# Two tile groups of the first layer norm turned by DMA, and a four-layer kernel's orders laid out anew

## The chip, the cores and the metric

The kernel runs on one core of a Trainium2 chip, in one launch. The metric is the device time of one execution in microseconds, and the figure for a kernel is the median of its timed runs. TensorE is called PE here, VectorE DVE, ScalarE ACT, GpSimd POOL, and SyncE, which issues the DMAs, SP.

## The reference

Two linear-attention layers and two feed-forward layers alternate on x (1 x 2048 x 512, bf16), each with a layer norm in front and a residual behind it.

```python
def _A_ref(x, wqkv, wo):                      # attention, 32 heads of 16
    q, k, v = ...                             # x @ wqkv
    phi = lambda t: jnp.where(t > 0, t + 1, jnp.exp(t)) + 1e-6
    pq, pk = phi(q), phi(k)
    kv = jnp.einsum("bhsd,bhse->bhde", pk, v)
    z = jnp.einsum("bhsd->bhd", pk)
    num = jnp.einsum("bhqd,bhde->bhqe", pq, kv)
    den = jnp.einsum("bhqd,bhd->bhq", pq, z)[..., None] + 1e-6
    ...                                       # (num / den) @ wo
def _B_ref(x, w1, w2):                        # relu(x @ w1) @ w2, inner width 1376
    ...
x = A_x
x = x + _A_ref(_layernorm(x, axis=-1), A_wqkv, A_wo)
x = x + _B_ref(_layernorm(x, axis=-1), B_w1, B_w2)
x = x + _A_ref(_layernorm(x, axis=-1), A_wqkv, A_wo)
x = x + _B_ref(_layernorm(x, axis=-1), B_w1, B_w2)
```

## The kernel before

The 2048 tokens are 16 tiles of 128, in four chunks of four tiles (chunk 0 is tiles 0 to 3, chunk 1 is 4 to 7). The layers are numbered 0 to 3, and an operation's name carries its layer (`0.kproj6`).

**Layer 0, a tile's way.** A chunk of x is loaded to `xin` (`ld_x`). DVE takes mean and variance (`bnst`, `bnag`, L476 and L477) and adds the epsilon (`veps`), POOL raises it to the power of -1/2 (`rstd`, L883 for a single tile of chunk 0, L491 for two tiles of chunk 1; ACT does it for chunks 2 and 3), and DVE scales (`norm`, L519) into `xn`. For matmuls the tile must be turned, 512 features by 128 tokens, into `Tb`. In `transpose_pe` PE does that with four matmuls of 128 x 128 against an identity (`trp`, L556), and ACT or DVE takes the result out of PSUM (`trev`, L560 and L561). In `transpose_chunk` a DMA does it (`tr`, L539, issued by SP). `FIRST_PE_CHUNKS = 2` sends chunks 0 and 1 to PE and chunks 2 and 3 to DMAs. Chunk 0 goes faster: its tiles are only centred (`cent`, L887) before they are turned, and the factor `rstd` enters when the products leave PSUM; the scaled copy in `xn` (L932) follows later.

From `Tb` come k (`kproj`, one group of four 512-column matmuls a tile, `a_k`) and q (`qtok` by tile in chunk 0, `qproj` by feature block in the others, `a_q`). `phi_evac` brings them through phi: ACT writes a linear part (`_lin`, L583) and an exponential (`_exp`, L585), DVE takes a minimum (`_em`, L587) and a maximum (`_phi`, L594). With a name in `STT`, DVE does the linear part within the maximum (L591).

**The product with pk.** The kernel does not compute v. `a_g` multiplies the transpose of `xn` with pk = phi(k) and adds over all 16 tiles in PSUM (`g<half>_<block>_<chunk>`, 256 columns, or 512 for block 3, which also gives the sums z through a column of ones that POOL writes into `xn`, `onec`). The result, `GT`, meets `wv` (`kv`, then `kvmask`) and `wo` (`m`), which gives `Mf`. The denominators (`den`, 32-column matmuls) go through Ln and Exp on ACT (`lnd`, `rdc`) and are spread over partitions by DMAs (`spread`); DVE multiplies them into pq (`pqs`), and pq times `Mf` gives the layer's output (`fin`), to which `resid` adds x. wv is changed before use by subtracting its last row (`wvless`), which waits for `ld_wv` and `ld_wvl`.

**What sets the order.** Every operation is put in a graph with what it reads and writes and an assumed duration, and `_list_schedule` lays out each engine's queue: among operations that could start at once, the smaller priority comes first. `HINTS` moves the priority of single operations, and `SEQS` fixes the order of some at the head. At run time each engine works its queue in order and waits on semaphores. All matmuls but the turning and warm ones are recorded at L601.

**The head.** Before data are there PE runs nine 512-column matmuls on a zeroed tile `wrm` (L451, `warm`) and one of 256 columns (L454, `warm2`), which DVE's memset (L444) releases. SP issues the loads in this order: tile 0 of x, tiles 1 to 3, two halves of wk, chunk 1, wq, chunks 2 and 3, wv (L432), the last row of wv (L433), wo (L434); then the transposes.

Of the kernel before, what the change touches and what calls it, by code (L numbers as in the profile page):

```python
# [9 lines left out]
BF16 = mybir.dt.bfloat16  # L10
# [5 lines left out]
C_MM512 = 216.0  # L16
C_MM256 = 109.0
C_MM128 = 57.0
C_MM96 = 42.5
C_MM_SWITCH = 95.0  # L20
C_MMTINY = 30.0
C_ACT_PSUM = 495.0
# [25 lines left out]

HINTS = {"2.zcol": 36, "2.norm0": -300, "2.norm1": -300, "2.norm2": -300, "2.norm3": -300, "0.bnag8": 9, "0.bnst11": -2, "0.bnst12": 58, "0.den1": 288, "0.fin11_0": 83, "0.fin8_0": 93, "0.g0_2_0": 180,
# [6 lines left out]

SEQS = {
    "dve": ["bnst0", "bnag0", "cent0", "bnst2", "bnst1", "bnag2", "cent3", "bnag1", "cent2", "trev0b"],
    "act": ["mean_3", "trev0a", "sq_3", "trev3", "trev2", "trev1"],
    "pool": ["veps_0", "rstd_0", "veps_2", "veps_1", "rstd_1", "var_3"],  # L60
    "pe": ["trp0a", "warm2"],
}

STT = {"0.k10", "0.k6", "0.k9", "0.q3_2", "0.q3_3"}


class _Op:
    __slots__ = ("eng", "emit", "reads", "writes", "dur", "lat", "sdeps", "odeps", "idx",
                 "seq", "dma", "name", "t_start", "t_done", "issued", "pos", "alts", "late", "prio", "key", "lock")

    def __init__(self, eng, emit, reads, writes, dur, lat, dma, name):
        self.eng = eng
        self.emit = emit
        self.reads = reads
        self.writes = writes
        self.dur = dur
        self.lat = lat
        self.dma = dma
        self.name = name
        self.sdeps = []  # L80
        self.odeps = []
        self.alts = None
        self.seq = None
        self.t_start = None
        self.t_done = None
        self.issued = False
        self.late = 0.0
        self.lock = eng == DVE and dur < 345.0 and (name.endswith(("_em", "_phi")) or name[:4] in ("cent", "norm", "wvle"))


class _Graph:

    def __init__(self):
        self.ops = []
        self.last_w = {}
        self.readers = {}
        self.tile_ops = {}
        self.ntiles = 0
        self.layer = 0

# [5 lines left out]
    def add(self, eng, emit, reads=(), writes=(), dur=100.0, lat=0.0, dma=False, name=""):  # L106
        op = _Op(eng, emit, tuple(reads), tuple(writes), dur, lat, dma, name)
        op.idx = len(self.ops)
        op.key = "%d.%s" % (self.layer, name)
        op.prio = op.idx + HINTS.get(op.key, 0)  # L110
        deps = {}
# [36 lines left out]
def _list_schedule(ops, tile_ops, vbank, nbanks=8):  # L148
# [44 lines left out]
    while remaining:  # L193
# [45 lines left out]
        o.issued = True  # L239
        o.t_start = st  # L240
        for v in alloc_of.get(o.idx, ()):
            bsel = None
# [49 lines left out]
def build_kernel(nc, A_x, A_wqkv, A_wo, B_w1, B_w2, out, n_layers_pairs=2, A_PE_CHUNKS=0, windows=None,  # L292
                 WARM=9, SPLIT0=True, TAIL_SPLIT=True, LAST_HALVES=True, FIRST_PE_CHUNKS=2,
                 flex_strict=True, flex_bias_dve=0.0):
# [18 lines left out]
    with es:  # L313
# [41 lines left out]
        nhalf = sb("nhalf", [128, 4], F32)  # L355
        wrm = sb("wrm", [128, 512], BF16)
        onesf = sb("onesf", [128, 128], F32)
# [65 lines left out]
        wq_v = A_wqkv.rearrange("(c p) n -> p c n", p=128)  # L423
        ld_x(0, 1, lat=1550.0)
        for k in range(2):
            dma(lambda e, k=k: e.dma_start(wqkv[:, 2 * k:2 * k + 2, D:2 * D], wq_v[:, 2 * k:2 * k + 2, D:2 * D]),
                [], [("wk", k)], 1050.0 + 150.0 * k, "ld_wk%d" % k)
        ld_x(1, lat=1450.0)
        dma(lambda e: e.dma_start(wqkv[:, :, 0:D], wq_v[:, :, 0:D]), [], [("wq",)], 1550.0, "ld_wq")
        for t in range(2, NCH):  # L430
            ld_x(t)
        dma(lambda e: e.dma_start(wqkv[:, :, 2 * D:3 * D], wq_v[:, :, 2 * D:3 * D]), [], [("wv0",)], 1500.0, "ld_wv")  # L432
        dma(lambda e: e.dma_start(wvl[:], A_wqkv[D - 1:D, 2 * D:3 * D].broadcast_to([128, D])), [], [("wvl",)], 1850.0, "ld_wvl")  # L433
        dma(lambda e: e.dma_start(wo[:], A_wo.rearrange("(c p) n -> p c n", p=128)), [], [("wo",)], 1650.0, "ld_wo")  # L434
        nfull = NFC - 1 if FLAST < 128 else NFC
# [8 lines left out]
        g.add(DVE, lambda e: e.memset(wrm[:], 0.0), [], [("wrm",)], 150, name="ms_wrm")  # L444
        if WARM > 0:
            wt = alloc_bank()

            def _warm(e):
                last = None
                for k in range(WARM):  # L450
                    last = e.matmul(psv[:, wt, :], wrm[:, 0:128], wrm[:, :], start=True, stop=True)  # L451
                return last
            g.add(PE, _warm, [("wrm",)], [("ps", wt)], WARM * 427.0, name="warm")
            g.add(PE, lambda e: e.matmul(psv[:, wt, 0:256], wrm[:, 0:128], wrm[:, 0:256], start=True, stop=True),  # L454
                  [("wrm",)], [("ps", wt)], 213.0, name="warm2")
        g.add(POOL, lambda e: e.memset(onesf[:], 1.0), [], [("onesf",)], 200, name="ms_ones")
# [87 lines left out]
        def transpose_pe(i):  # L544
            dst = Tb[:, i, :, :].rearrange("p c t -> p (c t)")

            def part(c0, n, key, tag):
# [5 lines left out]
                def _emit(e):  # L553
# [3 lines left out]
                    return last  # L557
                g.add(PE, _emit, [("xn", i), ("ident",)], [("ps", b)], n * (107.0 if i in (0, 3) else C_MM128), name="trp" + tag)
                d = dst[:, 128 * c0:128 * (c0 + n)]
                act = (ACT, lambda e: e.activation(d, psb()[:, :], ACTF.Identity), C_ACT_PSUM if n == 4 else 300.0)  # L560
                dve = (DVE, lambda e: e.tensor_copy(d, psb()[:, :]), 400.0 if n == 4 else 270.0)  # L561
                alts = [act, dve] if n == 4 else [act] if c0 == 0 else [dve]
                g.add_flex(alts, [("ps", b)], [key], name="trev" + tag)
# [57 lines left out]
        def a_k(i):  # L621
            b = alloc_bank()
            for c0, n, key, tag in ((0, 2, "T0a", "a"), (2, 2, "T", "b")) if i == 0 and g.layer == 0 else ((0, 4, "T", ""),):
                mm_group(lambda c0=c0, n=n: [(psv[:, b, :], Tb[:, i, c, :], wqkv[:, c, D:2 * D], c == 0, c == 3, False)
                                             for c in range(c0, c0 + n)],
                         [(key, i)] + [("wk", k) for k in range(c0 // 2, (c0 + n) // 2)], [("ps", b)], n * C_MM512, "kproj%d%s" % (i, tag))
            phi_evac(b, pk_tile(i), ("big", pk_unit(i)), "k%d" % i,
                     tok=i if g.layer == 0 and i < 4 else None)
# [18 lines left out]

        def a_g(m, i0, n, hf, GB, col, opens, width=256):
            def mk():
                mms = []  # L650
                for i in range(i0, i0 + n):
# [4 lines left out]
            mm_group(mk, [("xn", i) for i in range(i0, i0 + n)] + [("big", pk_unit(i)) for i in range(i0, i0 + n)],  # L656
                     [("ps", GB)], n * (C_MM256 if width == 256 else C_MM512), "g%d_%d_%d" % (hf, m, i0 // 4))

# [232 lines left out]
        def ln_first(t):  # L891
            if t == 0:
# [69 lines left out]
        def layer_steps(layer):  # L962
# [3 lines left out]
            if layer % 2 == 0:  # L966
# [237 lines left out]
```

## Time and profile before

| | before |
|---|---|
| timed runs, us | 280.75, 281.76, 282.42 |
| median, us | 281.76 |
| profiled execution, us | 280.62 |
| its span in the trace, us | 278.9 |
| PE busy, of the span | 98% |
| ACT, DVE, POOL busy | 61%, 52%, 17% |

The span runs from the first to the last instruction recorded; the rest of the profiled execution's time, 1.72 us, lies around it. In rows of the timeline the first number is the start and the second how long the row lasts, both in us; a row with xN is N instructions in one, and the bracket behind it is the engine's idle time before it and what ended that. Busy times of PE overlap from one matmul to the next, so the pace of matmuls is read from start to start.

### The profile page before, as it was taken

The numbers are of one execution on the slowest core, as the hardware profiler recorded it, in microseconds if no ns is written. First come the engines' busy times: TensorE is split into PE (matmuls) and PEld (weight loads), VectorE is DVE, ScalarE is ACT, GpSimd is POOL, SyncE is SP. The second block draws the span as 40 slices with busy tenths as digits, with TensorE's granted clock in tenths as the row PEclk, the third lists the DMA queues.
The fourth block names the chain that finished last, engine by engine and source line by source line (L and its number), as shares of the span: only waits on it lengthen the run. The fifth ranks groups of instructions, "written<-read, shape, count | busy, mean of one in ns | idle before, by whom it ended". The sixth has DMA issues, their size and how long they took to land.

```text
span 278.9 us, 4192 instructions
## 1 busy us (share of the span) xinstructions
PE 272.7 (98%) x1551; PEld 140.4 (50%) x1573; DVE 144.4 (52%) x385; ACT 169.5 (61%) x351; POOL 47.9 (17%) x131
## 2 busy tenths in 40 slices
PE   6999999999999999999999999999999999999996
PEld 2545656546544544544454455764654554454443
DVE  5999982899501362443363477379966300120222
ACT  4999787758773682678372799765683366226000
POOL 5500000044500160400040400005236100000000
PEclk9999999999999999999999999999999999999999
DMA  7922397655750043070006030084313641021012
GB/s 214 379 55 53 75 251 254 150 130 76 144 47 0 2 94 75 1 96 0 0 2 76 0 75 2 6 200 99 76 38 59 165 80 21 0 75 22 0 75 75
DMA packets 46356, 22.62 MB, mean 81 GB/s; under 512 B 36640, under 2 KB 44800, under 8 KB 46336
## 3 DMA queue, kind: packets, MB, share of 16 engines
q1 hardware_dynamic: 46336, 22.35, 35.3%
q8 instruction: 12, 0.20, 0.3%
q14 instruction: 8, 0.07, 0.1%
HBM read 7.14 MB, written 2.10 MB: 33 GB/s over the span
## 4 chain that ended last, share of the span: by engine, by line
PE 95%; DMA 1%; ACT 1%; issue 1%; DVE 1%; SPq 0%
PE ps L601 95%; DMA xin<-in_A_x_dram 1%; PE ps L556 1%; ACT big L583 1%; ACT escr L585 0%; DVE bst L476 0%; SPq L420 0%; DVE xn L932 0%; DVE xin L850 0%; DVE xn L887 0%; DVE mv L477 0%
## 5 line engine op out<-in xcount | busy, mean ns | idle before, releaser
L601 PE MATMUL ps<-w,big 128*128 128x512 bf16 (+4 forms) x355 | 76.2, 373 | 0.4
L601 PE MATMUL ps<-Tb,w 128*128 128x512 bf16 (+1 forms) x352 | 70.8, 360 | 0.0
L601 PEld LDWEIGHTS ps<-w,big 128*128 128x128 bf16 (+1 forms) x363 | 35.1, 98 | 41.1
L830 ACT ACTIVATE big<-ps 128x512 bf16<-128x512 f32 x67 | 40.0, 597 | 23.8 <-PE ps L601 23.5
L618 ACT ACTIVATE sqscr<-xres 128x512 bf16<-128x512 f32 x48 | 29.9, 623 | 36.5 <-DVE xres L612 36.2
L601 PEld LDWEIGHTS ps<-Tb,w 128*128 128x128 bf16 x352 | 33.9, 98 | 32.8
L612 DVE SCALAR_TENSOR_TENSOR xres<-ps,xres 128x512 f32<-128x512 f32 x32 | 21.2, 689 | 40.5 <-PE ps L601 40.5
L609 DVE TENSOR_TENSOR xin<-ps,xres 128x512 bf16<-128x512 f32 x15 | 10.4, 691 | 49.7 <-PE ps L601 49.7
L583 ACT ACTIVATE big<-ps 128x512 bf16<-128x512 f32 x51 | 32.0, 631 | 5.3 <-PE ps L601 5.3
L601 PE MATMUL ps<-wqkv,Tb 128*128 128x512 bf16 x138 | 32.6, 379 | 1.4 <-ACT Tb L560 1.0
L601 PE MATMUL ps<-big,xn 128*128 128x256 bf16 (+1 forms) x222 | 30.6, 287 | 0.1
L585 ACT ACTIVATE escr<-ps 128x512 bf16<-128x512 f32 x44 | 27.9, 636 | 1.0 <-PE ps L601 1.0
L601 PE MATMUL ps<-Tb,wqkv 128*128 128x512 bf16 x112 | 26.5, 379 | 0.1
L601 PEld LDWEIGHTS ps<-big,xn 128*128 128x128 bf16 x224 | 21.6, 98 | 8.8 <-issue 0.4
L601 PE MATMUL ps<-Mf,big 128*128 128x512 bf16 x109 | 24.8, 379 | 0.2
L587 DVE TENSOR_SCALAR escr<-escr 128x512 bf16<-128x512 bf16 x52 | 14.7, 290 | 17.8 <-ACT escr L585 17.8
L499 POOL TENSOR_SCALAR mean<-s 128x4 f32<-128x4 f32 (+1 forms) x13 | 3.1, 238 | 117.3 <-DVE xres L612 117.1
L601 PEld LDWEIGHTS ps<-wqkv,Tb 128*128 128x128 bf16 x144 | 13.8, 98 | 16.8 <-ACT Tb L560 1.2
L594 DVE TENSOR_TENSOR big<-big,escr 128x512 bf16<-128x512 bf16 x49 | 20.4, 421 | 1.1
L523 DVE TENSOR_SCALAR xn<-xres,mean,rstd 128x512 bf16<-128x512 f32 x24 | 16.1, 706 | 4.6 <-POOL nbias L513 4.3
L601 PEld LDWEIGHTS ps<-Mf,big 128*128 128x128 bf16 x112 | 10.7, 98 | 13.1 <-DVE big L755 0.4
L601 PEld LDWEIGHTS ps<-Tb,wqkv 128*128 128x128 bf16 x112 | 10.9, 98 | 11.6
(94 smaller groups left out, 227.8 us busy)
## 6 DMA issues: line engine op xcount, KB each, us to landing
big<-rdc SPq DMA_DIRECT2D x32, 128.0 KB, 2.7
xin<-in_A_x_dram SPq DMA_DIRECT2D x3, 512.0 KB, 7.4
w<-in_B_w_dram SPq DMA_DIRECT2D x1, 1376.0 KB, 7.9
w<-in_B_w_dram SPq DMA_DIRECT2D x1, 1280.0 KB, 10.7
wqkv<-in_A_wqkv_dram SPq DMA_DIRECT2D x2, 512.0 KB, 7.9
out_dram<-xin SPq DMA_DIRECT2D x2, 512.0 KB, 2.8
wqkv<-in_A_wqkv_dram SPq DMA_DIRECT2D x2, 256.0 KB, 4.1
wo<-in_A_wo_dram SPq DMA_DIRECT2D x1, 512.0 KB, 9.1
```

The source lines that it names most:

```text
L499: g.add(POOL, lambda e: e.tensor_scalar(mean[:, sl], s1[:, sl], -INV_D, None, ALU.mult), [("s1", i) for i in tl], [("mean", i) for i in tl ...
L523: ts = (POOL, lambda e: e.tensor_scalar(xn[:, i, :], src, mean[:, i:i + 1], rstd[:, i:i + 1], ALU.add, ALU.mult), C_POOL_NORM)
L556: last = e.transpose(psb()[:, 128 * c:128 * c + 128], xn[:, i, 128 * (c0 + c):128 * (c0 + c) + 128], ident[:])
L583: g.add(ACT, lambda e: e.activation(dst_ap, psv[:, b, :], ACTF.Identity, bias=1.0 + 1e-6, scale=sc), [("ps", b)] + rk, [dst_key], C_ACT_PS ...
L585: g.add(ACT, lambda e: e.activation(esc, psv[:, b, :], ACTF.Exp, scale=sc), [("ps", b)] + rk, [ekey], C_ACT_EXP + xd, name=name + "_exp")
L587: g.add(DVE, lambda e: e.tensor_scalar(esc, esc, 1.0, 1e-6, ALU.min, ALU.add), [ekey], [ekey], C_DVE_BF4X, name=name + "_em")
L594: g.add(DVE, lambda e: e.tensor_tensor(dst_ap, dst_ap, esc, ALU.max), [dst_key, ekey], [dst_key], 340.0, name=name + "_phi")
L601: last = e.matmul(o, l, r, start=st, stop=sp, skip_group_check=skip)
L609: g.add(DVE, lambda e: e.tensor_tensor(xin[:, i, :], psv[:, b, :], src, ALU.add), [("ps", b), skey], [("xin", i)], C_DVE_PSUM, name="resid ...
L612: g.add(DVE, lambda e: e.scalar_tensor_tensor(xres[:, i, :], psv[:, b, :], 0.0, src, ALU.add, ALU.add, accum_out=s1[:, i:i + 1]), [("ps", ...
L618: g.add(ACT, lambda e: e.activation(sqscr[:, q, :], xres[:, i, :], ACTF.Square, accum_out=s2[:, i:i + 1]), [("xres", i)], [("sqscr", q), ( ...
L830: g.add_flex([(ACT, lambda e, M=M, b=b, u=u: e.activation(unit_ap(u, M), psv[0:M, b, :], ACTF.Relu), C_ACT_PSUM), (DVE, lambda e, M=M, b=b ...
```

## The change

- `FIRST_PE_CHUNKS` is 1: chunk 1 is scaled and then turned by two DMAs of two tiles (`tr1_1` for tiles 6 and 7, `tr1_0` for 4 and 5, in that order on SP), and chunks 2 and 3 by two each. Sixteen turning matmuls and four evictions go. Chunk 1's statistics come in the order 6, 7, 4, 5.
- Chunk 0's part of the first product is cut in two pairs, tiles 0 and 2, then 3 and 1 (`g0_3_0p0` and so on). PE's queue: k of tiles 0, 3, 2, the turn of tile 1, q of 0 and 2, k of 1, q of 3 and 1, products of the first pair, k of 6, products of the second pair with others, k of 7, products, k of 4 and 5.
- wv, its last row and wo are issued behind chunk 1's transposes.
- The warm matmuls read a constant tile of ones that exists at the start, so nothing is waited for: eight of 512 columns, the turn of half of tile 0, five of 256 columns, the turn of the other half. Both evictions of tile 0 are on ACT, and the first k projection comes behind the turns of tiles 3 and 2.
- `HINTS`, `SEQS`, `STT` and some assumed durations are new, and with them all orders; of those far from the head, `den0`, `den1` and `den2` of layer 0 now stand together on PE, and in layer 2 the priorities of the first norms are gone.

```diff
-                 WARM=9, SPLIT0=True, TAIL_SPLIT=True, LAST_HALVES=True, FIRST_PE_CHUNKS=2,
+                 WARM=8, SPLIT0=True, TAIL_SPLIT=True, LAST_HALVES=True, FIRST_PE_CHUNKS=1,
...
-        dma(lambda e: e.dma_start(wqkv[:, :, 2 * D:3 * D], wq_v[:, :, 2 * D:3 * D]), [], [("wv0",)], 1500.0, "ld_wv")
...
-        g.add(DVE, lambda e: e.memset(wrm[:], 0.0), [], [("wrm",)], 150, name="ms_wrm")
...
+            one_w = nc.const_aps.tensor(1.0, [128, 128], BF16)
+            one_m = nc.const_aps.tensor(1.0, [128, 512], BF16)
...
+            warm([512] * WARM, "warm")
+            warm([256], "warm2")
+            for k in (3, 4, 5, 6):
+                warm([256], "warm%d" % k)
...
-            step = 2 if t < FIRST_PE_CHUNKS else 4
+            step = 2 if t < 2 else 4
...
-                tr_dma(t, 2 if t == 2 else 1)
+                tr_dma(t, 2)
+                if t == 1:
+                    load_out_weights(g.ops[-2:])
...
-        FIRST_ORDER = (0, 3, 1, 2)
+        FIRST_ORDER = (0, 2, 3, 1)
+        G_PAIRS = (FIRST_ORDER[:2], FIRST_ORDER[2:])
...
+                def g_pair(k):
+                    a_g(3, k, 2, 0, GR, 0, True, 512)
+                    for m in range(3):
+                        a_g(m, k, 2, 0, GA[m // 2], 256 * (m % 2), m % 2 == 0)
...
-                    if t >= 1:
+                    if t == 1 and first_layer:
+                        for k in range(len(G_PAIRS)):
+                            g_pair(k)
+                    elif t >= 1:
                         g_r(t - 1)
                         g_a(t - 1)
```

More of the change, by code (lines that the diff above doesn't have):

```diff
@@ L20 @@
 C_MM_SWITCH = 95.0
+C_DEN = 218.0
+T_CLK = 5600.0
 C_MMTINY = 30.0
@@ L98, in __init__ @@
         self.ntiles = 0
+        self.keys = set()
         self.layer = 0
@@ L240, in _list_schedule @@
         o.t_start = st
+        if e == PE:
+            if o.key.startswith("0.den"):
+                o.dur = C_DEN if order[PE][-1].name.startswith("den") else C_DEN + 2 * C_MM_SWITCH
+            o.wdur = o.dur
+            if st < T_CLK and o.key[:5] in ("0.trp", "0.kpr"):
+                o.dur *= 2.0
         for v in alloc_of.get(o.idx, ()):
@@ L443, in _table, with warm, _warm @@
             return e.activation(lnw[:], nhalf[:, 0:2], ACTF.Square)
-        g.add(DVE, lambda e: e.memset(wrm[:], 0.0), [], [("wrm",)], 150, name="ms_wrm")
         if WARM > 0:
             wt = alloc_bank()
[L448 to L455, printed above, removed]
+            one_w = nc.const_aps.tensor(1.0, [128, 128], BF16)
+            one_m = nc.const_aps.tensor(1.0, [128, 512], BF16)
+            def warm(cols, name):
+                def _warm(e):
+                    last = None
+                    for n in cols:
+                        last = e.matmul(psv[:, wt, 0:n], one_w, one_m[:, 0:n], start=True, stop=True)
+                    return last
+                g.add(PE, _warm, [], [("ps", wt), ("wrm",)], sum(cols) / 1.2, name=name)
+            warm([512] * WARM, "warm")
+            warm([256], "warm2")
+            for k in (3, 4, 5, 6):
+                warm([256], "warm%d" % k)
         g.add(POOL, lambda e: e.memset(onesf[:], 1.0), [], [("onesf",)], 200, name="ms_ones")
@@ L622, in a_k @@
             b = alloc_bank()
[L623 removed]
+            for c0, n, key, tag in ((0, 2, "T0a" if i == 0 else "T", "a"), (2, 2, "T", "b")) if i in FIRST_ORDER[:2] and g.layer == 0 else ((0, 4, "T", ""),):
                 mm_group(lambda c0=c0, n=n: [(psv[:, b, :], Tb[:, i, c, :], wqkv[:, c, D:2 * D], c == 0, c == 3, False)
                                              for c in range(c0, c0 + n)],
[L626 removed]
+                         [(key, i)] + [("wk", k) for k in range(c0 // 2, (c0 + n) // 2)] + ([("wrm",)] if g.layer == 0 else []), [("ps", b)], n * C_MM512, "kproj%d%s" % (i, tag))
             phi_evac(b, pk_tile(i), ("big", pk_unit(i)), "k%d" % i,
@@ L648, in a_g @@
         def a_g(m, i0, n, hf, GB, col, opens, width=256):
+            tl = range(i0, i0 + n) if n == 4 else G_PAIRS[i0]
             def mk():
                 mms = []
-                for i in range(i0, i0 + n):
+                for i in tl:
                     u = pk_unit(i)
@@ L655, in mk @@
                 return mms
-            mm_group(mk, [("xn", i) for i in range(i0, i0 + n)] + [("big", pk_unit(i)) for i in range(i0, i0 + n)],
-                     [("ps", GB)], n * (C_MM256 if width == 256 else C_MM512), "g%d_%d_%d" % (hf, m, i0 // 4))
+            mm_group(mk, [("xn", i) for i in tl] + [("big", pk_unit(i)) for i in tl],
+                     [("ps", GB)], n * (C_MM256 if width == 256 else C_MM512), "g%d_%d_%d" % (hf, m, i0 // 4) + ("" if n == 4 else "p%d" % i0))
         def a_g_evac_row(GR):
@@ L917, in ln_first, with load_out_weights @@
             if t >= FIRST_PE_CHUNKS:
-                tr_dma(t, 2 if t == 2 else 1)
+                tr_dma(t, 2)
+                if t == 1:
+                    load_out_weights(g.ops[-2:])
             ones_col(t)
-        FIRST_ORDER = (0, 3, 1, 2)
+        def load_out_weights(after):
+            n = len(g.ops)
+            dma(lambda e: e.dma_start(wqkv[:, :, 2 * D:3 * D], wq_v[:, :, 2 * D:3 * D]), [], [("wv0",)], 1500.0, "ld_wv")
+            dma(lambda e: e.dma_start(wvl[:], A_wqkv[D - 1:D, 2 * D:3 * D].broadcast_to([128, D])), [], [("wvl",)], 1850.0, "ld_wvl")
+            dma(lambda e: e.dma_start(wo[:], A_wo.rearrange("(c p) n -> p c n", p=128)), [], [("wo",)], 1650.0, "ld_wo")
+            for o in g.ops[n:]:
+                o.odeps.extend(after)
+        FIRST_ORDER = (0, 2, 3, 1)
+        G_PAIRS = (FIRST_ORDER[:2], FIRST_ORDER[2:])
         tr_state = {"first": True}
```

33 lines of the change are left out of this document (17 added, 16 removed), and 16 rows, old and new, of the table HINTS.

## The prediction

> **What bounds the kernel now.** I read the busy table first, then the chain that ended last, then the waits of TensorE (PE), and last the timeline of the first 20 us.
>
> ```profile
> PE 272.7 (98%) x1551; PEld 140.4 (50%) x1573; DVE 144.4 (52%) x385; ACT 169.5 (61%) x351; POOL 47.9 (17%) x131
> PE 95%; DMA 1%; ACT 1%; issue 1%; DVE 1%; SPq 0%
> PE ps L451 <- DVE wrm L444: 1.2, 1, 1.2
> PE ps L601 <- ACT Tb L560: 1.0, 1, 1.0
> PE ps L556 <- DVE xn L887: 0.3, 1, 0.3
> ```
>
> PE is busy for 98% and carries 95% of the chain. The three waits are all it has, and all lie ahead of 7 us. So from there on the kernel is one unbroken row of matmuls: a change can win what it removes from PE's work or from the head, and loses every wait that it brings in. Other engines matter only where they make PE wait.
>
> ```profile
> 1.24 3.40 PE L451 MATMUL ps<-wrm 128*128 128x512 bf16 x9 [1.24 <-DVE wrm L444]
> 2.92 0.15 PEld L451 LDWEIGHTS ps<-wrm 128*128 128x128 bf16 x1 [0.28 <-issue]
> 3.35 0.15 PEld L451 LDWEIGHTS ps<-wrm 128*128 128x128 bf16 x1 [0.28 <-issue]
> 4.97 0.63 ACT L897 ACTIVATE sqscr<-xin 128x512 bf16<-128x512 bf16 x1 [2.42 <-DMA xin<-in_A_x_dram]
> 4.97 1.29 DVE L476 BATCH_NORM_STATS2 bst<-xin 128x6 f32<-128x512 bf16 x2 [0.78 <-DMA xin<-in_A_x_dram]
> 5.60 0.36 ACT L560 ACTIVATE Tb<-ps 128x256 bf16<-128x256 bf16 x1
> 6.02 0.60 PE L601 MATMUL ps<-wqkv,Tb 128*128 128x512 bf16 x2 [1.05 <-ACT Tb L560]
> 6.17 0.40 DVE L932 TENSOR_SCALAR xn<-xin,mv,rstd 128x512 bf16<-128x512 bf16 x1
> 6.49 0.17 DVE L477 BATCH_NORM_AGGREGATE mv<-bst 128x2 f32<-128x6 f32 x1
> 6.58 0.32 DVE L887 TENSOR_SCALAR xn<-xin,mean 128x512 bf16<-128x512 bf16 x1
> 6.91 0.32 DVE L887 TENSOR_SCALAR xn<-xin,mv 128x512 bf16<-128x512 bf16 x1
> 6.96 0.72 PE L556 MATMUL ps<-ident,xn 128*128 128x128 bf16 x8 [0.34 <-DVE xn L887]
> 7.52 0.59 PE L601 MATMUL ps<-wqkv,Tb 128*128 128x512 bf16 x2
> 8.17 5.34 PE L601 MATMUL ps<-wqkv,Tb 128*128 128x512 bf16 x23
> ```
>
> The head is set by data: tiles 1 to 3 of x land, DVE takes their statistics from 4.97, centres tile 3 at 6.58 and tile 2 at 6.91, and PE turns them at 6.96. At 8.17 PE has turned four tiles and done one k projection; after that it never stops.
>
> **The change, part by part.** Prices of steady PE work, and of the handed-over steps:
>
> ```profile
> 15.53 0.61 PE L556 MATMUL ps<-ident,xn 128*128 128x128 bf16 x8
> 15.97 2.75 PE L601 MATMUL ps<-wqkv,Tb 128*128 128x512 bf16 x12
> 29.80 1.03 PE L601 MATMUL ps<-Tb,wqkv 128*128 128x512 bf16 x4
> 30.67 1.04 PE L601 MATMUL ps<-big,xn 128*128 128x256 bf16 x8
> 31.54 1.03 PE L601 MATMUL ps<-Tb,wqkv 128*128 128x512 bf16 x4
> 8.40 1.29 DVE L476 BATCH_NORM_STATS2 bst<-xin 128x6 f32<-128x512 bf16 x2 [0.19 <-DMA xin<-in_A_x_dram]
> 11.11 0.16 DVE L483 TENSOR_SCALAR veps<-mv 128x2 f32<-128x2 f32 x1
> 11.35 1.66 POOL L491 TENSOR_TENSOR rstd<-veps,nhalf 128x2 f32<-128x2 f32 x2 [1.61 <-DVE mv L477]
> 12.57 0.72 DVE L519 TENSOR_SCALAR xn<-xin,mv,rstd 128x512 bf16<-128x512 bf16 x2
> 19.37 0.75 DVE L594 TENSOR_TENSOR big<-big,escr 128x512 bf16<-128x512 bf16 x2
> 18.83 2.72 SPq L539 DMA_TRANSPOSE Tb<-xn  x2
> DMA to landing us min/median/max: 3.2/3.5/4.2
> ```
>
> From start to start, eight turning matmuls take 0.44 us (15.53 to 15.97), four of 512 columns 0.87 us (29.80 to 30.67), eight of 256 columns 0.87 us (30.67 to 31.54).
>
> *Removed.* Tiles 4 to 7 cost 16 turning matmuls: 2 x 0.44 = 0.88 us of PE, all on the path. Their four evictions on DVE and ACT were off it and count for nothing.
>
> *Head.* In the new order PE no longer starts the first k projection at 6.02 but after the turns of tiles 3 and 2, and DVE's scaling of tile 0 (the row at 6.17, 0.32 us to the next start at 6.49) stands behind both centrings. So tile 3 is centred at 6.26 and turned at about 6.64, tile 2 is centred at about 6.59 to 6.92 and turned at 6.98, and the first k projection starts at 6.98 + 0.22 = 7.20. Its input is there: on ACT the two evictions of tile 0 stand on both sides of the square of tile 3, and end by 6.9. At 7.20 PE has turned three tiles (0.66 us), and at 8.17 before it had turned four and done a projection (0.88 + 0.87 = 1.75). The new order thus stands at 7.20 - 0.66 = 6.54 against 8.17 - 1.75 = 6.42: 0.12 us behind. With the 0.88 us removed that is -0.76 us, if nothing waits.
>
> *Warm matmuls.* They start without the wait on DVE's memset, at an estimated 0.9 to 1.0 (that memset was issued at 0.91), and five of 256 columns follow tile 0's first turn. Nothing useful on PE is ready before 6.6, so they cost nothing; they would if the clock stayed low past 6.6, which I bound at the five themselves: 5 x 0.21 = 1.07 us at the low rate, ending near 5.7, so still 0.9 us inside the idle time.
>
> *The new wait.* From 7.20 PE has eight groups of 0.87 (four k, four q projections) and one turned tile, 0.22: 14.35 us. Then come product matmuls of tiles 0 and 2 (two of 512, six of 256 columns: 1.08 us), then the k projection of tile 6, which needs the DMA. PE is in order: all that is queued behind it waits too.
>
> First the product. On DVE I lay the new order end to end from x of chunk 1 at 8.40: two statistics 1.2, two small ones 0.2, a minimum of 0.2, a scaling 0.33, two more statistics 1.2, scalings of 6, 7 and 1 with small ones between 1.1, and then one statistic and the two maxima (0.33 each, the row at 19.37): the second maximum ends near 14.5. PE is 0.18 us early there.
>
> Then the DMA. Variances of 6 and 7 are ready at 10.46, POOL's power takes 0.83 (half of 1.66) and ends near 11.4, DVE reaches tile 6 at 11.7 and ends tile 7 at 12.5. SP has been idle, and issues at 12.5. Landing took 3.5 us for the first half chunk (18.83; median of the row) and 3.2 for the least: 15.7 to 16.0, or 16.7 by the longest, which is a whole chunk. I take 3.5, the half chunk issued to a quiet queue. PE is ready at 14.53 + 1.08 = 15.6 and starts at 16.1: 0.54 us of stall. Both stalls together: 0.72 us, between 0.2 (least landing, maxima on time) and 1.4 (longest).
>
> The other half (tiles 4 and 5) is scaled by 15.1 and lands by 18.6; PE gets there, after k of 6 and 7 and two more groups of products, at 19.8. The PSUM banks that k of 4 to 7 need are emptied by ACT with 0.2 us or more to spare by the same kind of count. These are covered; if ACT falls behind by more, the excess is stall.
>
> *Loads.*
>
> ```profile
> 4.70 0.54 SPq L432 DMA_DIRECT2D wqkv<-in_A_wqkv_dram  x1
> 5.28 1.18 SPq L433 DMA_DIRECT2D wvl<-in_A_wqkv_dram  x1
> 6.51 0.50 SPq L434 DMA_DIRECT2D wo<-in_A_wo_dram  x1
> 44.42 0.38 PE L601 MATMUL ps<-big,xn 128*128 128x256 bf16 x2
> 44.73 0.40 PE L601 MATMUL ps<-xres,Zc 128*32 128x512 bf16 x4
> 44.96 0.39 PE L601 MATMUL ps<-big,Zc 128*32 128x512 bf16 x4
> 195.76 1.00 DVE L523 TENSOR_SCALAR xn<-xres,mean,rstd 128x512 bf16<-128x512 f32 x2 [0.26 <-POOL rstd L509]
> 196.79 1.23 SPq L539 DMA_TRANSPOSE Tb<-xn  x1
> 199.99 0.50 PE L601 MATMUL ps<-w,Tb 128*128 128x96 bf16 x8
> ```
>
> wv, its last row and wo are issued behind the two transposes: 2.2 us of SP from about 16.5. The next on SP is tiles 10 and 11, by the same count scaled near 21.8; so the loads hide (if they did not, each microsecond would delay those tiles' projections, which I count at 25.9, 0.6 us behind the landing). Gone from ahead of the transposes, they leave the DMA queues quiet at 12.5, which is why 3.5 us can hold.
>
> *The orders.* Three denominators stand together now, where one stood alone. Going over from 256-column matmuls cost 0.31 - 0.22 = 0.09 us at 44.42 to 44.73, and coming back I take as much: one pair less is -0.19 us. In the second attention layer DVE puts two products (0.33 each) more ahead of the scaling of tiles 2 and 3, less 0.26 of idle time: 0.4 us later than 195.76. Their transpose then goes out at 197.2; the one of before was issued at 196.79 and met matmuls at 199.99 that had little slack. I take 0.2 us of stall, between 0 and 0.4.
>
> *Sum against the profiled execution (280.62 us):* -0.76 + 0.72 - 0.19 + 0.20 = -0.03 us. That execution lies 1.14 us under the median, 281.76.
>
> **The clock.** Warm weight loads at 2.92 and 3.35 are 0.43 us apart, twice the 0.216 of later 512-column matmuls, so PE starts at half rate; by 7.52 it runs at full rate. When it opens in the other runs no profile here shows. The new head has less idle PE time ahead of 5.7 than the old one; I credit 0.3 us of the 1.14, between 0 and all. The Trainium skill, "TensorE: Matmul & The Clock Gate" (Part 1: The HAM clock gate), says that the gate is judged in free-running windows of about 3.4 us, so that the point of opening moves from run to run. The trace agrees as far as one run can, with full rate some 3 us after 1.24.
>
> The forecast is 281.76 - 0.03 - 0.3 = **281.4 us**.
>
> **Rivals.**
> - *The clock was the spread (faster).* If late opening makes the median of before, and the filled head prevents it, all 1.14 us go; with the stalls at their least (0.2 for 0.72) the time is 281.76 - 0.03 - 1.14 - 0.52 = 280.1, and with 0 instead of 0.2 in the second layer 279.9. For it: eight projections at half rate would lose more than the spread of three runs (280.75 to 282.42). Against: nothing shows the clock in those runs. Chance 0.28.
> - *The transpose is late (slower).* k of tile 6 holds PE's queue, and each microsecond late is one lost. With the longest landing, 4.2, it is 0.7 more; with a late x of chunk 1 or a slow power on POOL, 1 us more: 281.4 + 1.7 = 283.1. It decides from a landing at about 17.9, 5.4 us after issue. For it: no slack at that place. Against: 3.2 and 3.5 at the only half chunks of the same stage. The Trainium skill, "VectorE: DVE Perf Modes" (The three transpose paths), speaks against the change: it lists 1309 ns for a 128 x 128 DMA transpose against 390 on TensorE; eight blocks one after another would be an estimated 10.5 us. The trace does not agree: eight blocks landed in 3.2 and 3.5 us. Chance 0.16.
> - *The forecast*, small gains eaten by two small waits: 0.56.
>
> A measurement of this kernel tells about 0.5% (1.4 us) from no change. The forecast's own bounds (stalls 0.2 to 1.4 and 0 to 0.4, clock 0 to 1.14) give 280.0 to 282.6; to hold 8 in 10 the range reaches 279.7 to 283.2. Chances: faster 0.28, same 0.56, slower 0.16.
>
> **What would show it.** In the new profile: no turning matmuls behind the fourth tile's; a first k projection at 7.2; a wait of PE on the transposes' DMA near 15.6 of about half a microsecond; none of size later but some 0.2 us at the start of the last feed-forward layer. A landing past 17 us, ACT evictions that PE waits for, or a first projection past 8 us would each make the forecast wrong, and so would a clock that opens later than 7 us.

## The result, and the profile after

| | before | changed |
|---|---|---|
| median, us (22 runs each) | 281.15 | 280.38 |
| lowest to highest, us | 280.45 to 283.36 | 279.71 to 281.15 |
| profiled execution, us (span) | 280.62 (278.9) | 280.69 (279.0) |

The ratio is 0.9972, 95% interval 0.9961 to 0.9983: some 0.8 us faster, less than the half per cent that the prediction called telling. A second measurement of the same changed kernel, among the experiments, gave 0.9985 (0.9970 to 1.0000), 0.2 us faster in the medians. The two profiled executions are equal: the one of before lies 0.53 us under its kernel's median, the changed one 0.31 above its own.

The busy table, the chain and PE's waits of the changed kernel:

```profile
PE 274.7 (98%) x1560; PEld 139.7 (50%) x1560; DVE 142.6 (51%) x382; ACT 167.5 (60%) x347; POOL 47.5 (17%) x131
PE 90%; DVE 5%; DMA 4%; SPq 1%; issue 0%
PE ps L466 <- PEq L1227: 0.8, 1, 0.8
PE ps L618 <- DMA wqkv<-in_A_wqkv_dram: 0.6, 2, 0.5
PE ps L573 <- DVE xn L906: 0.3, 1, 0.3
PE ps L618 <- DMA Tb<-xn: 0.2, 1, 0.2
```

PE's share of the chain went from 95% to 90%; DVE and DMA took it over. Before had no wait of PE behind 7 us. Now there are several, and the timeline shows where (start, duration, engine, line, what; in brackets the idle time ahead and who ended it):

```profile
4.25 1.28 DVE L493 BATCH_NORM_STATS2 bst<-xin 128x6 f32<-128x512 bf16 x2
6.47 0.59 PE L618 MATMUL ps<-wqkv,Tb 128*128 128x512 bf16 x2
7.23 2.33 PE L618 MATMUL ps<-wqkv,Tb 128*128 128x512 bf16 x10 [0.16 <-DMA wqkv<-in_A_wqkv_dram]
8.78 1.29 DVE L493 BATCH_NORM_STATS2 bst<-xin 128x6 f32<-128x512 bf16 x2 [1.36 <-DMA xin<-in_A_x_dram]
9.40 0.39 PE L573 MATMUL ps<-ident,xn 128*128 128x128 bf16 x4
10.26 4.49 PE L618 MATMUL ps<-wqkv,Tb 128*128 128x512 bf16 x20 [0.48 <-DMA wqkv<-in_A_wqkv_dram]
12.78 3.80 SPq L556 DMA_TRANSPOSE Tb<-xn  x2
14.28 0.40 DVE L611 TENSOR_TENSOR big<-big,escr 128x512 bf16<-128x512 bf16 x1
14.73 0.98 PEld L618 LDWEIGHTS ps<-big,xn 128*128 128x128 bf16 x8 [0.47 <-DVE big L611]
16.01 0.55 PEld L618 LDWEIGHTS ps<-wqkv,Tb 128*128 128x128 bf16 x4 [0.30 <-DMA Tb<-xn]
24.89 1.03 PE L618 MATMUL ps<-big,xn 128*128 128x512 bf16 x4
26.08 1.25 PE L618 MATMUL ps<-wqkv,Tb 128*128 128x512 bf16 x5 [0.17 <-DMA Tb<-xn]
67.11 0.50 PE L618 MATMUL ps<-w,Tb 128*128 128x96 bf16 x8
```

The waits are read at the matmuls' pace (0.216 us for 512 columns), for the brackets count only the time in which PE is shown idle. PE waits for the second half of wk: two matmuls from 6.47 end at 6.90, the next starts at 7.23, so 0.33. Then for wq: four turning matmuls of 0.055 from 9.40 end at 9.62, the next starts at 10.26, so 0.64. Then for the product's maps: 20 matmuls from 10.26 end at 14.58, the next starts at 14.73, so 0.15. For the k of tile 6: 14.73 + 1.08 = 15.81 against 16.01, 0.20. For chunk 2's transposes: 24.89 + 0.87 = 25.76 against 26.08, 0.32. That is 1.64 us of waits. The 0.88 us of matmuls taken out went into them, and with it a lead: the first k projection starts at 6.47 with three tiles turned (0.66 us), so the head stands at 6.47 - 0.66 = 5.81, by the prediction's way of counting, against before's 6.42.

The last row is the first matmul of the first feed-forward layer. In before it is this:

```profile
67.03 0.85 PE L601 MATMUL ps<-w,Tb 128*128 128x96 bf16 x16
```

From there to the end it is 278.9 - 67.03 = 211.9 us before and 279.0 - 67.11 = 211.9 after. Everything behind 67 us is worth the same in both orders; the whole question lies in the first attention layer.

### The profile page after: what moved, and what is told of

Its sections match the earlier page's. It is cut to its first block, busy times and chain, and to the rows that moved or that the text cites. A ratio compares the mean times of both kernels' runs of the same rounds, so it can differ in the third digit from the quotient of the medians.

```text
span 279.0 us, 4194 instructions
## 1 busy us (share of the span) xinstructions
PE 274.7 (98%) x1560; PEld 139.7 (50%) x1560; DVE 142.6 (51%) x382; ACT 167.5 (60%) x347; POOL 47.5 (17%) x131
## 4 chain that ended last, share of the span: by engine, by line
PE 90%; DVE 5%; DMA 4%; SPq 1%; issue 0%
PE ps L618 90%; DMA xin<-in_A_x_dram 2%; DVE bst L493 2%; DMA Tb<-xn 2%; DVE xn L536 1%; DVE big L611 0%; DVE escr L604 0%; SPq L442 0%; SPq L436 0%; DVE mv L494 0%; DVE xn L962 0%; DVE big L608 0%; DVE xin L869 0%; DVE veps L500 0%
## 5 line engine op out<-in xcount | busy, mean ns | idle before, releaser
L618 PE MATMUL ps<-w,big 128*128 128x512 bf16 (+3 forms) x363 | 77.4, 373 | 0.0
L618 PE MATMUL ps<-wqkv,Tb 128*128 128x512 bf16 x144 | 33.4, 379 | 0.8 <-DMA wqkv<-in_A_wqkv_dram 0.6
L618 PE MATMUL ps<-big,xn 128*128 128x256 bf16 (+1 forms) x224 | 31.8, 288 | 0.0
```

The costliest lines, as they stand in the source:

```text
L618: last = e.matmul(o, l, r, start=st, stop=sp, skip_group_check=skip)
```

## The experiments

Theories. *Matmuls pace the head* (the prediction's sum): what is taken from PE is gained, and each wait of PE is lost. *Data pace the head*: x's chunk 1, DVE's row of work behind it and the transposing DMAs set the time, and PE's work only fills it. *The clock*: the new warm matmuls bring the gain. The ratios are to before, whose median in these three groups of runs was 281.22 (the first four), 280.89 (the next four) and 280.81 (the last four). In the titles: ratio, interval, median.

### The warm matmuls alone, on the kernel before: 0.9990 (0.9973 to 1.0007), 280.83 us

```
-  for k in range(WARM): e.matmul(psv[:, wt, :], wrm[:, 0:128], wrm[:, :], ...)
+  for k in range(8): e.matmul(psv[:, wt, :], one_w, one_m, ...)
...
+  for k in range(5): e.matmul(psv[:, wt, 0:256], one_w, one_m[:, 0:256], ...)
```

> The kernel before in its own order, with nothing changed but the warm matmuls: eight 512-wide and five 256-wide on the constant tile, waiting for nothing, in place of nine and one on a tile that a memset zeroes first. If the warm matmuls cost and bring nothing, as the prediction has it, the ratio to before is 1.000 (within 0.001). If the lower median of the changed kernel (0.9972 of before) comes from its warm matmuls, by an earlier or steadier full clock, this kernel has it too: 0.997, and its runs lie within 1.5 us of each other as those of the changed kernel do, not 2.9.

### The old warm matmuls in the changed kernel: 0.9984 (0.9968 to 0.9999), 280.54 us

```
-  one_w = nc.const_aps.tensor(1.0, [128, 128], BF16)
+  g.add(DVE, lambda e: e.memset(wrm[:], 0.0), ...); one_w = wrm[:, 0:128]
-  warm([512] * WARM, "warm")
+  warm([512] * 9, "warm")
```

> The changed kernel with the warm matmuls of before (nine 512-wide and one 256-wide on a zeroed tile, behind the memset). If the warm matmuls are the source of the gain, it goes: ratio 1.000, and the spread is wide again. If the gain lies in the transposes and the order of the head, it stays: 0.997.

With the old warm matmuls the changed kernel does as well as with its own (0.9985 in its second measurement), and before's time does not measurably change with the new ones. The clock theory as the main cause falls, though not to the last 0.3 us: the interval of the first kernel reaches 0.9973, and the second had its orders laid out anew, with another order on DVE from 17 us on and no wait for chunk 2's transposes in its trace:

```profile
25.59 1.89 PE L618 MATMUL ps<-wqkv,Tb 128*128 128x512 bf16 x8
```

Whether the new ones narrow before's spread (11 of 12 runs within 0.7 us, against 1.9 us for 23 of before), these are too few runs to say.

### Two DMAs alone, on the kernel before: 1.0331 (1.0307 to 1.0356), 290.34 us

```
-  FIRST_PE_CHUNKS=2,
+  FIRST_PE_CHUNKS=1,
-  tr_dma(t, 2 if t == 2 else 1)
+  tr_dma(t, 2 if t <= 2 else 1)
```

> The kernel before with one part of the change alone: tiles 4 to 7 turned by two DMAs of two tiles each in place of 16 matmuls, with the order laid out anew; the product in whole steps, the loads of wv and wo and the warm matmuls as before. The prediction's terms: -0.88 us of matmuls, +0.12 behind the head, and the waits for the DMA (0.2 to 1.4), so -0.6 to +0.6 us, ratio 0.998 to 1.002. If the transposes' DMAs queue behind wv and wo, which land up to 15.6 us here, they land late and it is slower, 1.004 or more. If the removed matmuls are the source of the whole gain, 0.997.

A miss of all theories: 9 us slower. The timeline, and a table of stretches (window, its length, busy time of PE, PEld, DVE, ACT and POOL, then the granted clock, the DMA share and GB/s):

```profile
PE ps L601 <- DVE big L594: 7.2, 2, 5.8
13.89 15.86 SPq L539 DMA_TRANSPOSE Tb<-xn  x5
19.49 0.42 DVE L594 TENSOR_TENSOR big<-big,escr 128x512 bf16<-128x512 bf16 x1
20.06 1.01 PE L601 MATMUL ps<-big,xn 128*128 128x256 bf16 x4 [5.82 <-DVE big L594]
17.00:20.00 3.00, 0.00 (x0) 0.00 (x0) 3.00 (x11) 1.43 (x4) 0.33 (x2) 0.92 0.33 63
20.00:22.00 2.00, 1.94 (x7) 1.05 (x8) 2.00 (x7) 0.00 (x0) 0.00 (x0) 0.50 0.93 181
22.00:24.00 2.00, 2.00 (x8) 0.79 (x7) 1.18 (x6) 1.18 (x3) 0.12 (x1) 0.77 0.44 82
```

The product in whole steps waits for the last map of chunk 0, which DVE makes at 19.49, behind the norms of chunks 1 and 2. Before makes its maps no earlier (a pair of them is the row at 19.37 in the prediction), but there PE turns and projects tiles 4 to 7 first and comes to its first product at 22.02:

```profile
22.02 1.90 PE L601 MATMUL ps<-big,xn 128*128 128x256 bf16 x11
```

In the order laid out for the two DMAs the k of tiles 4 to 7 stands behind the product, so nothing is in front of it, and PE idles 5.8 us. The idling costs twice: at its end and for some 3 us behind it the granted clock is down, to 0.50 at 20 to 22 us. With a second wait of the same kind (1.3 us) and one of 1.1 for `xres` further on, PE's waits behind 14 us add up to 8.3 us, and the low clock takes some 1.5 us more (2 x 0.50 and 2 x 0.23).

### The changed kernel with tiles 4 to 7 turned by TensorE: 1.0166 (1.0141 to 1.0192), 285.78 us

```
-  FIRST_PE_CHUNKS=1,
+  FIRST_PE_CHUNKS=2,
```

> The changed kernel with tiles 4 to 7 turned by TensorE again (16 matmuls, about 0.88 us, in place of the two DMAs), and wv and wo loaded right behind x; warm matmuls and pairs as changed. If the removed matmuls carry the gain, it goes: 1.000 of before, perhaps 1.001. If the warm matmuls or the pairs carry it, it stays at 0.997.

It says little of the turning, for the order laid out for it lost its time elsewhere, from 57 us on:

```profile
59.69 1.89 PE L618 MATMUL ps<-Mf,big 128*128 128x512 bf16 x6 [2.68 <-DVE big L774]
60.00:65.00 5.00, 4.78 (x16) 1.91 (x16) 4.32 (x12) 2.84 (x7) 1.60 (x4) 0.66 0.34 73
```

Up to its first product with Mf it is level with the changed kernel (52.51 against 52.42 us) with 16 more matmuls, though chunk 1 of x came earlier in that execution (8.12 against 8.78), which leaves the comparison open. Then one wait of 2.7 us, and the low clock behind it. From here on I mostly kept the changed kernel's order and moved single things in it.

### The k of tile 6 without its wait: 0.9991 (0.9976 to 1.0006), 280.76 us

```
+  src = 0 if i == 6 and g.layer == 0 else i
-  Tb[:, i, c, :]
+  Tb[:, src, c, :]
```

> The changed kernel in its own order, but the first layer's k of tile 6 is computed from tile 0's turned data, so that its matmuls wait for nothing of the DMA (the k of that one tile is left out; the matmuls are the same in number and size). It gives the price of that wait. The prediction put it at 0.54 us (0.2 to 1.4); the profile of the changed kernel shows 0.2 to 0.3. So 0.001 of the time below the changed kernel: 0.996 of before. If what waits there waits anyway for the next thing, the same 0.997.

Nothing is won that these runs can tell. The wait is gone at 16 us, and at 21 us PE is 0.09 us ahead of the changed kernel, though chunk 1 of x came 0.11 later in that execution (8.89); then it stands at the next DMA, and is 0.04 behind:

```profile
26.12 1.25 PE L618 MATMUL ps<-wqkv,Tb 128*128 128x512 bf16 x5 [0.29 <-DMA Tb<-xn]
```

### The loads of wv and wo ahead of the transposes: 1.0019 (1.0007 to 1.0032), 281.42 us

```
+  late = [o for o in order[SP] if o.key in ("0.ld_wv", "0.ld_wvl", "0.ld_wo")]
+  k = [o.key for o in rest].index("0.ld_x3_0") + 1
+  order[SP] = rest[:k] + late + rest[k:]
```

> The changed kernel in its own order, but the loads of wv and wo are issued right behind x, ahead of the two transposing DMAs, as in the kernel before. If the transposes' landing doesn't depend on them, 0.997 of before, as the changed kernel. If they share the engines' time with 1.5 MB of loads, the first transpose lands one to two us later than 15.8, and TensorE waits that much: 1.001 to 1.004 of before, which is the slower rival of the prediction made to happen.

```profile
17.04 1.04 PE L618 MATMUL ps<-wqkv,Tb 128*128 128x512 bf16 x4 [1.13 <-DMA Tb<-xn]
DMA to landing us min/median/max: 3.2/3.7/4.3
```

The two transposes now take 3.2 to 4.3 us from issue to landing instead of 3.1 and 3.2 in the changed kernel, and the k of tile 6 starts 1.03 us later. At 26 us it is only 0.70 later, because the wait for chunk 2's transposes has gone with the loads. So the "transpose is late" rival is real, and a microsecond of it costs 0.7 in the profiled execution, and 0.9 to 1.3 us by the ratios (1.0019 against 0.9985 and 0.9972). The loads are 1.1 MB by the profile's rows (512, 128 and 512 KB), not the 1.5 of the expectation.

### Chunk 0's product in whole steps: 1.0023 (1.0010 to 1.0036), 281.69 us

```
-  if t == 1 and first_layer: g_pair(0), g_pair(1)
-  elif t >= 1:
+  if t >= 1:
```

> The changed kernel with the product of chunk 0 in whole steps again (it waits for all four tiles' maps) and the order laid out anew. With pairs, half of the product fills TensorE while the first transpose is under way. If that filling is worth the wait it covers, this is slower by about 0.5 to 1 us: 0.999 to 1.001 of before. If the order finds other work for that place, no difference: 0.997.

```profile
16.18 1.04 PE L618 MATMUL ps<-wqkv,Tb 128*128 128x512 bf16 x4 [1.26 <-DMA Tb<-xn]
```

Slower by 1.1 to 1.4 us than the changed kernel (0.9985 and 0.9972): without the pairs there is nothing to put in front of the k of tile 6, and its wait is 1.26 us where PE waited 0.15 and 0.20. The k itself starts no later, counted from x (8.96 in that execution); what is lost is that the product, 1.08 us, now stands behind it.

### Chunk 1 of x in halves, order laid out anew: 1.0153 (1.0131 to 1.0176), 285.27 us

```
-  ld_x(1, lat=1750.0)
+  ld_x(1, 2, 4, lat=875.0)
   dma(... "ld_wq")
+  ld_x(1, 0, 2, lat=875.0)
```

> The changed kernel with chunk 1 of x loaded in two halves, tiles 6 and 7 ahead of wq and tiles 4 and 5 behind it, and the order laid out anew. Tiles 6 and 7 and wq should come some 0.5 us earlier, and with them the first transpose and the q projection (which wait 0.2 and 0.5 in the profile of the changed kernel). If the landing times are what is left at the head, 0.2 to 0.5 us below the changed kernel: 0.9955 of before. If the next matmuls wait for the other half instead, 0.997 to 0.999.

Inconclusive, like the turning by TensorE, and for a like reason: PE waits 2.5 us for DVE's `big` (L775) between the layers, and 1.2 us for DVE's maps (L612) at the head.

```profile
8.77 1.29 DVE L494 BATCH_NORM_STATS2 bst<-xin 128x6 f32<-128x512 bf16 x2 [1.34 <-DMA xin<-in_A_x_dram]
PE ps L619 <- DVE big L775: 2.5, 1, 2.5
PE ps L619 <- DVE big L612: 1.2, 2, 0.9
```

The first row is a miss of its own: tiles 6 and 7, loaded ahead of wq as half a chunk, are taken up at 8.77, no earlier than in the changed kernel.

### The changed kernel again: 0.9985 (0.9970 to 1.0000), 280.59 us

> The changed kernel itself, unaltered, for comparison with the three kernels beside it on one chip, and for a second trace. If its gain is one of structure, the ratio is 0.997 again and the profiled run lies at 280.4. From the traces so far: TensorE's last 212 us are the same in every kernel of this order, so the time differs only by when the first feed-forward part of layer 1 begins (66.6 to 67.2 us).

The ratio is compatible with the first, 0.9972. The profiled execution came out at 280.73, not the 280.4 expected, and repeats the first one nearly step for step: x at 8.75, the k of tile 6 at 15.98, the wait for chunk 2 at 26.10, the same span of 279.0.

### The changed kernel and 16 matmuls more: 0.9989 (0.9976 to 1.0003), 280.71 us

```
   last = e.transpose(...)                       # tile 1
+  if tag == "1":
+      for k in range(16):
+          last = e.matmul(psv[:, b, 256:384], one_w, one_m[:, 0:128], start=True, stop=True)
```

> The changed kernel in its own order with 16 matmuls of 128 columns on the constant tile (their results are read by nobody) put behind tile 1's turning, ahead of the wait for wq: as many as the change took away. If TensorE is what paces the head, as the prediction's sum has it, they give back 0.88 us: 1.003 of the changed kernel. If the head is paced by x's second chunk, VectorE and the transposing DMAs, TensorE has 0.48 of waiting at that place, 0.14 and 0.2 behind it and 0.3 at 26 us to absorb them in: 1.000 to 1.0005 of the changed kernel.

As many matmuls as the change took out, put back at this place, cost 0.12 us in the median, not 0.88 (280.71 against 280.59 for the changed kernel beside it). The two intervals leave some 0.6 us of room about that, so 0.88 is outside, though not by much. This is the result that tells the theories apart: the data pace the head, as the second said. It holds for this place, where all of PE's waits from wq on (1.31 us) lie ahead to take the matmuls in.

### The loads of wv and wo behind the transposes: 0.9982 (0.9969 to 0.9994), 280.42 us

```
+  move(SP, "0.ld_wv", "0.tr2_0"); move(SP, "0.ld_wvl", "0.ld_wv"); move(SP, "0.ld_wo", "0.tr3_1")
```

> The changed kernel in its own order, but wv's loads are issued behind the two transposes of chunk 2 and wo's behind those of chunk 3 (first use at 34.9 and 49.8 us). If the loads under way (wo lands at 25.0 us) hold up the transposes of chunk 2, TensorE's wait of about 0.3 at 26.1 us goes: 0.999 of the changed kernel. If that wait comes from VectorE's lateness alone, the same as the changed kernel; if the loads then hold up chunk 3's transposes, a wait appears behind 30 us and nothing is won.

In time this is not told apart from the changed kernel (0.17 us in the medians). The traces show the mechanism: in its profiled execution PE is 0.61 us behind the changed kernel at the product of 14.7 us, for x came late, and 0.30 behind from 26 us on. The wait for chunk 2's transposes is gone, and it is worth 0.31. Moving the loads is not the only way to lose it: in the kernel with the old warm matmuls they stand where the change put them, but wo lands at 24.1 us, not 25.0, and the wait is missing too.

### Late loads, and chunk 1 of x in halves: 0.9958 (0.9941 to 0.9975), 279.90 us

```
+  xa.emit = _x_part(6, 8, xa.seq)           # tiles 6 and 7
+  xb = dma(... xin[:, 4:6, :] ..., "ld_x1_b")  # tiles 4 and 5, next in order[SP]
```

> The kernel of the late loads, with chunk 1 of x loaded as two halves, tiles 6 and 7 first, in the changed kernel's own order. VectorE waits 1.36 us for that chunk in the profile of the changed kernel (until 8.78 us). If that landing paces the head, tiles 6 and 7 come 0.3 to 0.4 us earlier and all that hangs on them: 0.998 of the changed kernel, the best version. If TensorE's own work or wq paces it, no difference to the kernel of the late loads; if one more DMA ahead of wq makes wq later, up to 0.3 us slower.

The best version: 0.9 us below before, 0.7 below the changed kernel and 0.5 below the late loads beside it, and its six runs lie within 0.5 us. The intervals of the two kernels with late loads just overlap (0.9969 to 0.9975).

```profile
7.91 1.29 DVE L493 BATCH_NORM_STATS2 bst<-xin 128x6 f32<-128x512 bf16 x2 [0.33 <-DMA xin<-in_A_x_dram]
10.05 4.49 PE L618 MATMUL ps<-wqkv,Tb 128*128 128x512 bf16 x20 [0.24 <-DMA wqkv<-in_A_wqkv_dram]
11.90 11.80 SPq L556 DMA_TRANSPOSE Tb<-xn  x4
15.46 1.03 PE L618 MATMUL ps<-wqkv,Tb 128*128 128x512 bf16 x4
25.19 1.89 PE L618 MATMUL ps<-wqkv,Tb 128*128 128x512 bf16 x8
66.21 0.50 PE L618 MATMUL ps<-w,Tb 128*128 128x96 bf16 x8
```

No wait of PE is left behind 10.05, where it still waits for wq. From there on the head is PE's own work, and it ends 0.82 us ahead of before's 67.03. That this is near the -0.76 that the prediction gave "if nothing waits" is chance: the first k starts at 6.58 and not at 7.20, and the 0.62 so won go into 0.64 of waits for wk and wq. Nor is all of the lead over the late loads' trace (67.41) the halves' doing: 0.78 of its 1.20 us stands when PE starts q (10.05 against 10.83), for wk and wq came earlier too in this execution; 0.41 are the waits for the product's maps and the k of tile 6, which are gone.

### What paces the head

Kernels that share the changed order up to the k of tile 6, by their profiled executions (us). The columns are when DVE takes up chunk 1 of x, when SP issues the first transpose, when PE starts the k of tile 6 and the k of chunk 2, when the first feed-forward layer starts, and the span:

| kernel | x | transpose | k of tile 6 | k of chunk 2 | feed-forward | span |
|---|---|---|---|---|---|---|
| late loads, x in halves | 7.91 | 11.90 | 15.46 | 25.19 | 66.21 | 278.1 |
| old warm matmuls | 8.62 | 12.61 | 15.85 | 25.59 | 66.61 | 278.5 |
| early loads | 8.71 | 12.71 | 17.04 | 26.78 | 67.80 | 279.7 |
| changed, again | 8.75 | 12.75 | 15.98 | 26.10 | 67.13 | 279.0 |
| changed | 8.78 | 12.78 | 16.01 | 26.08 | 67.11 | 279.0 |
| no wait at tile 6 | 8.89 | 12.89 | 15.93 | 26.12 | 67.15 | 279.0 |
| late loads | 9.40 | 13.40 | 16.64 | 26.39 | 67.41 | 279.3 |
| 16 matmuls more | 9.69 | 13.68 | 17.10 | 27.19 | 68.21 | 280.1 |

Four rows from the last kernel, the first of them its wait for the second half of wk:

```profile
8.37 2.33 PE L621 MATMUL ps<-wqkv,Tb 128*128 128x512 bf16 x10 [1.27 <-DMA wqkv<-in_A_wqkv_dram]
9.69 1.29 DVE L493 BATCH_NORM_STATS2 bst<-xin 128x6 f32<-128x512 bf16 x2 [2.23 <-DMA xin<-in_A_x_dram]
13.68 3.80 SPq L556 DMA_TRANSPOSE Tb<-xn  x2
68.21 0.50 PE L621 MATMUL ps<-w,Tb 128*128 128x96 bf16 x8
```

From x's take-up to the issue it is 4.0 us in every row, whatever PE did. In the changed kernel's two executions, the old warm matmuls and the late loads the k of tile 6 starts 7.23 to 7.24 us behind x, though x itself varies by 0.78: there x, DVE's row and the transposing DMA set the pace. (The early loads and the kernel without the wait at tile 6 change this very wait.) In the first and the last row it is more, 7.55 and 7.41, and PE comes to that k without a wait: there PE's own row is the later one. In the last row it started late, for the second half of wk was late as well (7.88 with the late loads and 8.37 here, against 7.23 in the changed kernel), and it had the 16 matmuls to do. Counted from x, its feed-forward layer starts 58.52 us behind, against 58.33 and 58.38 in the changed kernel: 0.14 to 0.19 for the 16 matmuls, which agrees with the 0.12 of the medians.

From the k of chunk 2 to the feed-forward layer it is 41.0 us in every row, and from there to the end 211.9. Between the two k's lies the wait for chunk 2's transposes, which some rows have and some do not: the old warm matmuls are 0.5 us ahead of the changed kernel by 0.13 of x and 0.4 of that wait.

What varies from execution to execution is the landing of the first loads. For the same loads in whole chunks x was taken up between 8.12 us (the kernel with the turning by TensorE) and 9.69, and wk and wq moved with it where it was late. The profiled run with the 16 matmuls is the slowest of its twelve (281.79 against a median of 280.71), and it has the latest x and wk. That these landings also spread the runs that left no trace here is inferred. For before, whose one profiled execution has x at 8.40 and no wait behind 7 us, the cause of its spread stays open, and with it where the 0.2 to 0.8 us in the medians come from: the two profiled executions are equal.

## Why the prediction was right or wrong

The total (281.4 forecast, 280.38 measured; no change that can be told) held, but by luck: the head came out 0.73 us better than forecast and the waits 0.9 us worse, and the two cancel.

- **The removed matmuls, -0.88, are mis-sized.** They are gone from PE's row, but most of their time was not gained: put back ahead of the wait for wq, they cost 0.12 us. The failing step is "from there on the kernel is one unbroken row of matmuls", carried over to the new head. It laid out PE's work from 7.20 to 14.35 without asking when wk and wq land. In the new head PE waits for the second half of wk until 7.23 and for wq until 10.26, 0.97 us together, and the sum had no term for either.
- **The head, +0.12.** The first k projection was put at 7.20 and started at 6.47, because tiles 1 to 3 were taken up at 4.25 in that execution and not at 4.97: -0.61 in place of +0.12, by when a load landed. The order of turns was as predicted. So -0.61 - 0.88 + 1.64 of waits is +0.15 at 26 us, where the prediction had -0.76 + 0.72 = -0.04; at the feed-forward layer it is +0.08.
- **The product's wait.** 0.18 predicted, 0.15 measured, by luck. The terms listed for DVE add up to 13.9, not 14.5, and by them nothing would wait. The second map ended at 14.68, 5.9 us behind x; from x at 8.40 that would be 14.3, level with PE's 14.35. The wait came of x's being 0.38 later than counted while PE, held by wq, was 0.23 later.
- **The DMA's wait.** Issue 12.5, start 16.1 and a stall of 0.54 were predicted; 12.78, 16.01 and 0.20 measured. The landing, 3.5 by the row, was 3.1 to 3.2. The price was wrong in kind, too: taking the wait away won nothing that can be told, since the next wait takes its place.
- **The other half** was met at 19.71 us (19.8 predicted) without a wait.
- **The loads, 0.** They cost 0.31 us in the profiled execution, by the experiments that moved them; in the medians that is not told from nothing. The prediction counted SP's 2.2 us of issuing, not that the bytes are still on their way (wo takes 7.2 us to land) when chunk 2's transposes are issued.
- **The later orders, -0.19 and +0.20.** Between 26 us, where the new order stands 0.15 behind, and 67 us, where it stands 0.08 behind, 0.07 is won and not 0.19. Behind 67 us there is no gain and no loss: 211.9 us in both, and no wait at the last feed-forward layer.
- **The clock, 0.3 of the 1.14.** The warm matmuls bring nothing that the two exchanges can tell. Of the 1.14, 0.61 was a median of three runs: over 22, before's is 281.15.
- **The range.** With its own bounds the lower end is 281.43 - 0.52 - 0.20 - 0.84 = 279.9, not 280.0.
- **The rivals.** That the clock made before's spread was not shown. The late transpose exists, and decides where the prediction put it, at 0.7 us for each us in the trace. On the Trainium skill's figure ("VectorE: DVE Perf Modes", The three transpose paths), which spoke against the change, eight blocks one after another would take an estimated 10.5 us (8 x 1309 ns); the DMA turned eight blocks in 3.1 to 3.2 us.

Two DMAs alone lose 9 us and the whole change wins a little. The whole change ends the maps that its first product needs at 14.68 us, where the two DMAs alone had the last one at 19.49; and its pairs give PE work while the DMA turns, worth 1.1 to 1.4 us. The first reading is from the traces: no run here has the new order of DVE's maps alone. The prediction priced the pairs' own wait and never what the order would cost without them.

## What to carry to other kernels

Where an engine is busy for 98%, work taken from it is won only up to the next thing that was just hidden: list when each load and each other engine's result arrives, and lay the shortened row against all of them, not only against the new wait. If putting the removed work back costs next to nothing, the pace is set elsewhere; here it was the landing of the first loads, above all one chunk of x. Splitting that chunk and issuing other loads later won 0.7 us more in the medians, against 0.2 to 0.8 for the change itself. And an order laid out anew can move a wait of 2.7 us to the other end of a layer: to price one edit, keep the order and move that edit alone.

## What the runs showed of the hardware

- After a long idle stretch of PE the granted clock fell. 5.8 us of idling were followed by 0.50 at 20 to 22 us. A wait of 2.68 us (the kernel with the turning by TensorE) was followed by a mean of 0.66 over 60 to 65 us, which is 5 x 0.34 = 1.7 us more lost; a wait of 2.49 us (chunk 1 of x in halves, order laid out anew) left it at 1.00 for the next 7.5 us. Waits of up to 1.3 us left it at 1.00 too.
- The same loads, issued at the same times, land up to 1.6 us apart from one execution to the next (x's chunk 1 taken up at 8.12 to 9.69 us), and that is about as much as the changed kernel's runs differ (1.4 us).
- A transposing DMA issued while loads are on their way can land late: 3.1 to 3.2 us from issue in the changed kernel's chunk 1, 4.3 for the first one with wv and wo issued ahead of it. In three traces the first transpose issued with wo under way landed about 1 us behind it: 17.0 against 16.0 with the early loads, 26.0 against 25.0 in the changed kernel's chunk 2, and 25.1 against 24.1 with the old warm matmuls, where that was only 3.0 us from its issue.
